# Sliding-window attention issued as 96 items, with row-tiled scores, one PSUM ring and the small transfers on SyncE

## The chip, the cores and the metric

The kernel runs on one core of one Trainium2 chip. The metric is the device time of one execution in microseconds, the median of several runs. The core has a matrix engine (TensorE, PE in the profile, with its weight loads as PEld), a vector engine (VectorE, DVE), an activation engine (ScalarE, ACT), GpSimd (POOL) and SyncE (SP), which here only issues DMA transfers. Each engine executes its own instructions in program order and waits on semaphores for the others.

## The reference

Two independent parts, each with 2048 positions and 576 channels, are computed and put side by side.

```python
# part A: 32 heads of 18, causal window of 256
qkv = (x @ wqkv).reshape(B, S, 3, H, Dh) ...          # q, k, v: [B, H, S, 18]
scores = einsum("bhqd,bhkd->bhqk", q, k) * Dh ** -0.5
mask = (i - j >= 0) & (i - j < 256)
p = softmax(where(mask, scores, -1e9))
a = einsum("bhqk,bhkd->bhqd", p, v) ... @ wo
# part B: a state-space filter with 128 states a channel, applied as a causal convolution by FFT
K[d, l] = real(sum_n C[d,n] * exp(dt * A[d,n] * l) * dt * B[d,n])
b = irfft(rfft(pad(u)) * rfft(pad(K)))[:L] + u * Dskip
out = concatenate([a, b], -1)
```

## The kernel before

The kernel has two stages. The first (to about 520 us) projects q, k and v (`proj`, written to `qd` and `vd` in HBM as pairs of f16 numbers that add up to one f32), builds the filter table K (`tables`) and makes the first half of the FFT of u and of K (`s1_u`, `s1_k`, written to `gx` and `gk` in HBM). The change does not touch it.

The second stage runs attention and the rest of the convolution side by side. Attention has 16 units: unit i is one half of the queries (1024) and one group of four heads. In a unit:

- `gmax_load` and `load_stacks` bring q, k and V from HBM. The f16 pairs are stacked on the partitions, so that one matmul of 54 rows and one further row computes a score with its row maximum taken off. The four heads lie side by side in a tile of 96 partitions.
- `gmax` finds an upper bound of each row's maximum: DVE spreads q into a block-diagonal tile `Qbd` (L580), PE multiplies 32 queries of four heads with 288 keys (L593) and adds a bias that hides the keys outside of the window (L596, L599), DVE reduces (L602 for a pair of two banks, L606 for the shorter ones). A transpose (L609) and a scaling (L611) turn the maxima into rows, and four transfers on POOL's queue (L613) put them into the tile Q.
- `att_chunk` computes, twice a unit, 512 queries: transposed scores of four heads (L634) in three banks of blocks listed in `BL`, the exponential on ACT (L636), the window's edges cut to zero on POOL (L645), and the products with V and a column of ones (L652), accumulated in `po`. DVE copies `po` into `osb` (L657).
- `norm` divides by the sum: transfers on POOL's queue gather the sums (`den`, L663), DVE inverts them (L664), they go out to HBM (`rd`, L666) and come back spread over partitions (`rb`, L669); DVE multiplies (L670), ACT and DVE split into an f16 pair (L672, L673), and POOL's queue stores it to `od` (L676).

The convolution (`conv`) has 16 passes over frequency pairs: loads, the second FFT half of u and K (L464), complex products on DVE (L486 to L489), sums (L494, L495), the inverse half (L497), a store to `h` on POOL's queue (L500). Then 16 steps of the last FFT (L517), each with four loads of `h` on SP, four of u and a product with Dskip on POOL, an addition on DVE (L519) and four stores. `wo` is the output projection (14 matmuls of 288 columns a tile, L151) and a scaling on ACT (L723); its first half may begin when units 0 to 7 are stored, its second when all are.

In the unit's loop, generators of attention, maxima of the next unit, convolution and projection are merged step by step (`merge`), with a share for each. What stands in the source is not yet the order on the engines: the compiler that the kernel is built with schedules the instructions once more before it fixes each engine's program, with pools of rotating buffers deciding what may overlap. Pools that matter: `sps` (maxima, one tile of two PSUM banks), `stp` (scores, one tile of two banks), `ops` (one bank, shared by `po` and the transpose), `fps` (three banks, convolution and projection), `P` (three tiles of exponentials).

Of the kernel before, what the change touches and what calls it, by code (L numbers as in the profile page):

```python
# [10 lines left out]
F32 = mybir.dt.float32  # L11
# [10 lines left out]
HQ = 1024  # L22
# [16 lines left out]
def constants():  # L39
# [33 lines left out]
    bd = np.zeros((96, 4))  # L73
    for j in range(4):
        bd[18 * j:18 * j + 18, j] = 1
    c["c_w1"], c["c_w2"], c["c_i1"], c["c_i2"] = w1, w2, i1, i2
    c["c_id"], c["c_bias"], c["c_bd"] = np.eye(128), bias, bd
# [14 lines left out]
def part(g, n):  # L92
    for _ in range(n):
        try:
            next(g)
        except StopIteration:
            return
        yield


class Kernel:
# [348 lines left out]
    def conv(self):  # L450
        nc, a, tt = self.nc, self.a, self.nc.vector.tensor_tensor
        fs, fy, fps = self.p["fs"], self.p["fy"], self.p["fps"]

        def gload(g, fp, nm, eng):
            t = fs.tile([128, 4, 2, 144], F32, name=nm)
            eng.dma_start(t, g.rearrange("a l (s f) j -> (a l) s f j", s=4)[:, :, 2 * fp:2 * fp + 2, :])
            return t

        def s2(w2, t, fp, hs):
            r = []  # L460
            for part in range(2):
                ps = fps.tile([128, 512], F32, name="fps")
                for par in range(2):
                    nc.tensor.matmul(ps[64 * par:64 * par + 64, :288], w2[:, par, 64 * part:64 * part + 64],  # L464
                                     t[:, 2 * hs:2 * hs + 2, par, :], start=True, stop=True)
                r.append(ps[:, :288])
            return r

        for fp in range(16):
            w2 = fs.tile([128, 2, 128], F32, name="w2")  # L470
            nc.sync.dma_start(w2, a["c_w2"][:, 2 * fp:2 * fp + 2])
            i1 = fs.tile([128, 2, 128], F32, name="i1")
            nc.sync.dma_start(i1, a["c_i1"][:, 2 * fp:2 * fp + 2])
            tx = gload(self.gx, fp, "tx", nc.sync)
            tk = gload(self.gk, fp, "tk", nc.sync)
            ho = fs.tile([128, 2, D], F32, name="ho")
            for hs in range(2):
                xr, xi = s2(w2, tx, fp, hs)
                X = fy.tile([128, 2, 288], F32, name="X")
                self.evac(X[:, 0], xr)  # L480
                self.evac(X[:, 1], xi)
                yield
                kr, ki = s2(w2, tk, fp, hs)
                t1 = fy.tile([128, 2, 288], F32, name="t1")
                t2 = fy.tile([128, 2, 288], F32, name="t2")
                tt(t1[:, 0], X[:, 0], kr, op=OP.mult)  # L486
                tt(t2[:, 1], X[:, 1], kr, op=OP.mult)  # L487
                tt(t2[:, 0], X[:, 1], ki, op=OP.mult)
                tt(t1[:, 1], X[:, 0], ki, op=OP.mult)  # L489
                yield  # L490
                for par in range(2):
                    Y = fy.tile([128, 288], F32, name="Y%d" % par)
                    sl = slice(64 * par, 64 * par + 64)
                    tt(Y[0:64], t1[sl, 0], t2[sl, 0], op=OP.subtract)  # L494
                    tt(Y[64:128], t1[sl, 1], t2[sl, 1], op=OP.add)  # L495
                    ps = fps.tile([128, 512], F32, name="fps")
                    nc.tensor.matmul(ps[:, :288], i1[:, par, :], Y, start=True, stop=True)  # L497
                    self.evac(ho[:, par, hs * 288:hs * 288 + 288], ps[:, :288])
                yield
# [3 lines left out]
        for qd in range(16):  # L503
# [5 lines left out]
            ut = fs.tile([128, D], F32, name="tx")  # L509
            y = fs.tile([128, D], F32, name="tk")  # L510
            for k in range(4):
                nc.gpsimd.dma_start(ut[32 * k:32 * k + 32], uw[4 * qd + k])
# [314 lines left out]
```

## Time and profile before

| | |
|---|---|
| median of 3 runs | 1375.21 us (1371.36 to 1375.58) |
| profiled execution | 1368.52 us, span 1366.8 us |
| mean granted PE clock | 0.828 |
| busy share of the span | PE 74%, PEld 39%, DVE 55%, ACT 44%, POOL 40% |

The span is the time from the first to the last instruction of the profiled execution; the execution took 1.7 us more. Busy time is the time in which an engine works on an instruction; matmuls are pipelined, and their ends are modelled, so busy PE is not PE at its peak. In a list of groups a row has line, engine, operation, output and input tile, shapes, count, then busy us and mean ns of one, then the idle time before them with what ended it. In a timeline or chain a row has start, duration, engine or queue, line and count. DMA transfers of SP have no landing time in this profile, those of POOL's queue have.

### The profile page before, as it was taken

How to read it: one execution, taken by the hardware profiler on the slowest of the kernel's cores; microseconds unless marked ns; L12 is line 12 of the kernel's file. 1: busy time of each engine (PE TensorE's matmuls, PEld its weight loads, DVE VectorE, ACT ScalarE, POOL GpSimd, SP SyncE). 2: the span in 40 equal slices, each digit the busy share in tenths (PEclk: the TensorE clock that was granted, in tenths of full speed). 3: DMA queues.
4: the chain of work that ended last, by engine and by line, in shares of the span. 5: the costliest groups of instructions: out<-in, count | busy, mean ns of one | idle time of the engine just before them, and what ended most of it. 6: DMA issues, size and time to landing. Idle time of an engine off the chain costs nothing.

```text
span 1366.8 us, 25524 instructions
## 1 busy us (share of the span) xinstructions
PE 1009.0 (74%) x10314; PEld 535.1 (39%) x10314; DVE 755.2 (55%) x1229; ACT 599.5 (44%) x879; POOL 549.1 (40%) x700
## 2 busy tenths in 40 slices
PE   1548898798889864876797789667888896666338
PEld 1224464464455532333343334333444453222116
DVE  4797667777753254566766677544555765411210
ACT  2867687687783320432343234422443352233002
POOL 0024343454450260244543354333534454576640
PEclk8659999999999986788888888757999997776559
DMA  9563142133125668144433444225344423434673
GB/s 269 141 181 103 34 116 75 54 75 98 50 56 153 168 179 229 52 128 113 125 117 107 127 125 146 84 65 143 87 114 137 140 75 109 105 88 118 160 177 130
DMA packets 155541, 162.34 MB, mean 119 GB/s; under 512 B 34752, under 2 KB 128512, under 8 KB 155232
## 3 DMA queue, kind: packets, MB, share of 16 engines
q1 hardware_dynamic: 138768, 128.65, 33.9%
q0 software_dynamic: 15152, 28.08, 7.2%
q10 hardware_dynamic: 1504, 3.99, 1.0%
q8 instruction: 81, 1.33, 0.4%
q14 instruction: 36, 0.29, 0.1%
HBM read 103.11 MB, written 57.15 MB: 117 GB/s over the span
## 4 chain that ended last, share of the span: by engine, by line
PE 43%; DVE 22%; DMA 14%; ACT 9%; issue 6%; POOL 5%; SPq 2%; ACTq 0%; DVEq 0%; POOLq 0%
PE po L652 7%; PE ST L634 6%; PE fps L464 5%; PE S L593 5%; PE pp L151 5%; DVE m L602 4%; DMA Q<-m 4%; PE fps L151 4%; ACT P L636 3%; PE fps L497 3%; PE kp L388 2%; PE pp L431 2%; DMA den<-osb 2%; DMA gk<-g 2%; DVE Qbd L580 2%
## 5 line engine op out<-in xcount | busy, mean ns | idle before, releaser
L636 ACT ACTIVATE P<-ST,esc 128x1024 f32<-128x1024 f32 (+1 forms) x192 | 203.5, 1060 | 270.3 <-PE ST L634 242.6
L602 DVE TENSOR_REDUCE m<-S 128x2 f32<-128x576 f32 x224 | 168.7, 753 | 163.1 <-PE S L596 161.4
L645 POOL TENSOR_SCALAR_AFFINE_SELECT P<-P 128x512 f32<-128x512 f32 x240 | 159.7, 695 | 199.5 <-ACT P L636 189.2
L350 POOL TENSOR_TENSOR m<-A,tr 128x1024 f32<-128x1024 f32 x72 | 149.5, 2098 | 193.5 <-PE kp L388 143.9
L593 PE MATMUL S<-kh,Qbd 96*128 96x288 f16 (+7 forms) x512 | 135.4, 323 | 87.4 <-DVE m L602 55.3
L634 PE MATMUL ST<-Q,K 96*128 96x384 f16 (+2 forms) x704 | 141.3, 320 | 65.4 <-ACT P L636 38.1
L652 PE MATMUL po<-P,V 128*32 128x256 f32 (+2 forms) x1408 | 132.9, 458 | 14.3 <-POOL P L645 13.1
L634 PEld LDWEIGHTS <-K 96*128 96x128 f16 x704 | 64.8, 108 | 150.5 <-issue 132.3
L388 PE MATMUL kp<-Q,m 128*32 128x64 f32 x4608 | 87.6, 229 | 27.5 <-DVE Q L371 10.5
L388 PEld LDWEIGHTS kp<-Q,m 128*32 128x32 f32 x4608 | 74.6, 115 | 55.6 <-issue 41.8
L593 PEld LDWEIGHTS <-Qbd 96*128 96x128 f16 x512 | 56.3, 111 | 97.1 <-issue 38.3
L596 PE MATMUL S<-bias,idb 128*128 128x64 bf16 x448 | 92.0, 216 | 0.0
L431 PE MATMUL pp<-ut,w 128*128 128x288 f32 x128 | 51.4, 526 | 42.2 <-DMA ut<-in_u_dram 24.9
L652 PEld LDWEIGHTS po<-P,V 128*32 128x32 f32 x1408 | 41.4, 122 | 82.1 <-issue 42.9
L596 PEld LDWEIGHTS <-idb 128*128 128x128 bf16 x448 | 47.9, 108 | 62.3 <-issue 59.3
L464 PE MATMUL fps<-tx,w 128*64 128x288 f32 x256 | 66.1, 456 | 0.0
L497 PE MATMUL fps<-Y,i 128*128 128x288 f32 x128 | 56.1, 537 | 11.1 <-DVE Y L495 6.3
L464 PE MATMUL fps<-tk,w 128*64 128x288 f32 x256 | 61.4, 430 | 0.4 <-DVE t L487 0.4
L517 PE MATMUL fps<-ho,i 128*64 128x288 f32 x128 | 29.7, 593 | 39.7 <-DMA ho<-h 33.3
L519 DVE TENSOR_TENSOR tk<-fps,tx 128x288 f32<-128x288 f32 x32 | 14.4, 457 | 73.6 <-PE fps L517 65.6
L114 ACT ACTIVATE X<-fps 128x288 f32<-128x288 f32 x64 | 25.8, 409 | 66.5 <-PE fps L464 62.1
L114 ACT ACTIVATE g<-pp 128x288 f32<-128x288 f32 (+1 forms) x84 | 34.5, 446 | 46.1 <-PE pp L431 25.3
(160 smaller groups left out, 1918.8 us busy)
## 6 DMA issues: line engine op xcount, KB each, us to landing
gx<-g SPq DMA_DIRECT2D x32, 288.0 KB
qd<-qst SPq DMA_DIRECT2D x36, 256.0 KB
gk<-g SPq DMA_DIRECT2D x16, 576.0 KB
tx<-gx SPq DMA_DIRECT2D x16, 576.0 KB
tk<-gk SPq DMA_DIRECT2D x16, 576.0 KB
h<-ho POOLq DMA_DIRECT2D x16, 576.0 KB, 3.6
ho<-h SPq DMA_DIRECT2D x64, 144.0 KB
raw<-in_xT_dram SPq DMA_DIRECT2D x16, 512.0 KB
```

What stands on the lines that cost most here:

```text
L151: self.nc.tensor.matmul(ps, u, v, start=(i == 0), stop=(i == len(ops) - 1))
L350: self.nc.gpsimd.tensor_tensor(m, A[:, ch, a0:a0 + 8].unsqueeze(3).to_broadcast(sh), tr[:, ch, part, 0:8].unsqueeze(2).to_broadcast(sh), o ...
L388: nc.tensor.matmul(kp[32 * st:32 * st + 32, c % 2 * JJ2 + j, :], m[:, ch, a0:a0 + 32], Q[:, ch, term % 2, :], start=(term == 0), stop=(ter ...
L464: nc.tensor.matmul(ps[64 * par:64 * par + 64, :288], w2[:, par, 64 * part:64 * part + 64], t[:, 2 * hs:2 * hs + 2, par, :], start=True, st ...
L497: nc.tensor.matmul(ps[:, :288], i1[:, par, :], Y, start=True, stop=True)
L593: nc.tensor.matmul(ps[:, u, :n[u]], bdt[:, t].rearrange("p j q -> p (j q)"), kh[:, k0:k1], start=True, stop=False, skip_group_check=True)
L596: nc.tensor.matmul(ps[:, u, :288].rearrange("p (a b) -> p a b", b=32)[:, 0:9:8], self.idb, self.bias, start=False, stop=True, skip_group_c ...
L602: nc.vector.tensor_reduce(m[:, 2 * sp:2 * sp + 2], ps[:, :, :n[0]], axis=AX.X, op=OP.max)
L634: nc.tensor.matmul(ps[:, u, o:o + n], d["K"][:, j, k0:k0 + 128], d["Q"][:, j, q0:q0 + n], start=True, stop=True, skip_group_check=True)
L636: nc.scalar.activation(pt[:, 2 * jp:2 * jp + 2, lo:hi], ps[:, :, lo:hi], AF.Exp, scale=self.esc)
L645: nc.gpsimd.affine_select(v, v, pattern=[[0, 4], [sg, 128]], compare_op=OP.is_ge, fill=0.0, base=-1 if far else 0, channel_multiplier=-sg)
L652: nc.tensor.matmul(po[32 * j:32 * j + 32, t0 * 128:t1 * 128], d["V"][:, kb * 76 + 19 * j:kb * 76 + 19 * j + 32], P[off // 512][:, j, o:o + ...
```

## The change

Attention becomes one generator, `attention`, that walks 96 items: one item is one bank of one chunk of one unit. In item n the scores of item n, the V products of item n-2, seven of the next unit's maxima steps, two or three of 225 smaller convolution steps and, from item 62, one projection step are merged. Besides:

- Scores are row-tiled: two heads lie in partitions 0 to 63 and 64 to 127, each with 64 rows, and the two matmuls of a pair use different halves of the rows and different banks. The number of score matmuls stays.
- `stp` has two tiles in place of one. `sps` and `fps` become one `ring` of three one-bank tiles for maxima, transpose, convolution and projection. `P` has four buffers, V three, `n` two.
- q is loaded straight into its block-diagonal tile, by four transfers with runs of 64 bytes, so DVE's spreading is gone; the reduces are all single (32 a unit).
- `po` is copied by ACT. `norm` yields twice, so that its steps lie an item apart.
- Transfers of the maxima, of `norm`, of `h` and of u go from POOL's queue to SP's. Convolution loads are issued one pass or one step ahead.
- Most of the memsets at the start of the stage move from POOL to DVE.

The core of the diff (the functions that only move text are left out):

```diff
     def gmax(self, i):
-        for sp in range(16):
-            ps = self.p["sps"].tile([128, 2, 512], F32, name="S")
...
+        for t in range(32):
+            ps = self.p["ring"].tile([128, 512], F32, name="r")
+            full = hf > 0 or t >= 8
+            k0 = 32 * t if full else 256
+            n = 32 * t + 288 - k0
+            nc.tensor.matmul(ps[:, :n], d["q"][:, t].rearrange("p j q -> p (j q)"), d["k"][:, k0:k0 + n],
+                             start=True, stop=False, skip_group_check=True)
...
+            nc.vector.tensor_reduce(m[:, t:t + 1], ps[:, :n], axis=AX.X, op=OP.max)
+            yield
+        yield
+        mt = self.p["ring"].tile([128, 512], F32, name="r")
         nc.tensor.transpose(mt[:32, :128], m, self.ident)
...
         for j in range(4):
-            nc.gpsimd.dma_start(d["Q"][64:65, j].rearrange("o (s q) -> o s q", q=32), m16[:, 32 * j:32 * j + 32])
+            r = 64 * (j % 2) + 54
+            nc.sync.dma_start(d["Q"][r:r + 1, j // 2].rearrange("o (s q) -> o s q", q=32), m16[:, 32 * j:32 * j + 32])
+    def scores(self, i, c, bank):
+        nc, d, bb = self.nc, self.sets[i % 2], self.blocks(i, c, bank)
+        pt = self.p["P"].tile([128, 4, 512], F32, name="P")
...
+        for jp in range(2):
+            ps = self.p["stp"].tile([128, 2, 512], F32, name="ST")
+            for off, r, t0, t1 in bb:
...
+                for u in range(2):
+                    h = slice(64 * u, 64 * u + 64)
+                    nc.tensor.matmul(ps[:, u, o:o + n], d["K"][h, jp, k0:k0 + 128], d["Q"][h, jp, q0:q0 + n],
+                                     start=True, stop=True, skip_group_check=True)
+            nc.scalar.activation(pt[:, 2 * jp:2 * jp + 2, lo:hi], ps[:, :, lo:hi], AF.Exp, scale=self.esc)
+            yield
...                                   # the window's edges on POOL, as before
+    def values(self, i, c, bank):
...                                   # the V products of one bank, as before
+        if bank == 2:
...
+            nc.scalar.activation(self.osb[i][:, c * 512:c * 512 + 512], self.po, AF.Copy)
+    def norm(self, i):
...                                   # as before, on nc.sync, with a yield after den and after rb
+    def attention(self, conv):
+        self.V, self.Pt, self.osb, norms = {}, {}, {}, []
+        self.load_unit(0)
+        for _ in self.gmax(0):
+            pass
+        items = [(i, c, b) for i in range(16) for c in range(2) for b in range(3)]
+        wo0 = self.wo(0)
+        for n in range(len(items) + 2):
+            streams = []
+            if n < len(items):
+                i = items[n][0]
+                if n % 6 == 0 and i < 15:
+                    self.load_unit(i + 1)
+                    gm = self.gmax(i + 1)
+                streams.append((self.scores(*items[n]), 2))
+                if i < 15:
+                    streams.append((part(gm, 7), 7))
+            if n >= 2:
+                streams.append((self.values(*items[n - 2]), 2))
+            k = conv_steps(n)                 # (n + 1) * 225 // 96 - n * 225 // 96
+            streams.append((part(conv, k), k))
+            if n == 24:
+                self.wo_load()
+            if n >= 62:
+                streams.append((part(wo0, 1), 1))
+            merge(*streams)
+            norms = [g for g in norms if next(g, 0) is None]
+            if n >= 2 and (n - 2) % 6 == 5:
+                norms.append(self.norm(items[n - 2][0]))
+                next(norms[-1])
...                                   # then the rest of norms, conv, wo0, and wo(1)
@@ build
-                for n, b, s in (("fs", 2, None), ("fy", 2, None), ("att", 1, None), ("bd", 1, None), ("m", 2, None),
-                                ("P", 3, None), ("v", 2, None), ("o", 2, None), ("n", 1, None), ("wo", 1, None),
-                                ("wo2", 2, None), ("sps", 1, PSUM), ("stp", 1, PSUM), ("ops", 1, PSUM),
-                                ("fps", 3, PSUM)):
+                for n, b, s in (("fs", 2, None), ("fy", 2, None), ("att", 1, None), ("m", 2, None), ("P", 4, None),
+                                ("v", 3, None), ("o", 2, None), ("n", 2, None), ("wo", 1, None), ("wo2", 2, None),
+                                ("stp", 2, PSUM), ("ops", 1, PSUM), ("ring", 3, PSUM)):
```

The convolution's steps become smaller (six instead of three yields for each half pass) and issue their loads first:

```diff
+        nx = load(0)
         for fp in range(16):
-            w2 = fs.tile([128, 2, 128], F32, name="w2")
...
+            cu, nx = nx, load(fp + 1) if fp < 15 else None
...
-            nc.gpsimd.dma_start(self.h.rearrange("a l f d -> (a l) f d")[:, 2 * fp:2 * fp + 2, :], ho)
+            nc.sync.dma_start(self.h.rearrange("a l f d -> (a l) f d")[:, 2 * fp:2 * fp + 2, :], ho)
...
+        nx = loadh(0)
+        yield
         for qd in range(16):
+            (hp, ut), nx = nx, loadh(qd + 1) if qd < 15 else None
```

More of the change, by code (lines that the diff above doesn't have):

```diff
@@ new lines, in ring, with s2 @@
+        def ring():
+            return self.p["ring"].tile([128, 512], F32, name="r")[:, :288]
+        def s2(w2, t, part, hs):
+            ps = ring()
+            for par in range(2):
+                nc.tensor.matmul(ps[64 * par:64 * par + 64], w2[:, par, 64 * part:64 * part + 64],
+                                 t[:, 2 * hs:2 * hs + 2, par, :], start=True, stop=True)
+            return ps
+        nx = load(0)
+        for fp in range(16):
+            cu, nx = nx, load(fp + 1) if fp < 15 else None
```

273 lines of the change are left out of this document (108 added, 165 removed).

## The prediction

> **What bounds the kernel now.** I read the page's span, then the windows, then PE's timeline for marks that cut the attention stage into units, and then the chain of waits inside one unit.
>
> ```profile
> span 1366.8 us, 25524 instructions
> 543.40:1227.60 684.20, 536.38 (x3839) 259.57 (x3839) 395.78 (x724) 248.04 (x307) 304.63 (x509) 0.82 0.39 109
> 543.37 0.39 PE L609 MATMUL po<-ident,m 128*32 128x128 f32 x1 [1.25 <-DVE m L602]
> 1227.61 0.28 PE L609 MATMUL po<-ident,m 128*32 128x128 f32 x1 [0.81 <-DVE osb L657]
> ```
>
> The transpose of the row maxima (L609) runs once a unit: fifteen cycles in 684.2 us, 45.6 us each. The columns after the length are PE, PEld, DVE, ACT, POOL, the clock and DMA. PE is busy 78% of it at 0.82 of the clock, DVE 58%, ACT 36%: no engine is full, so order and waits set the time. Two waits stand out, in the chain of a unit that has little else to do, and in the timelines of POOL and ACT at a unit's border.
>
> ```profile
> 1237.87 1.02 PE ST L634 x4
> 1238.92 1.12 ACT P L636
> 1240.08 1.02 PE ST L634 x4
> ...
> 849.80 2.06 POOL L663 DMA_DIRECT2D den<-osb  x4 [1.53 <-DVE V L560]
> 851.85 0.98 POOL L613 DMA_DIRECT2D Q<-m  x2
> 859.05 1.00 POOL L613 DMA_DIRECT2D Q<-m  x2
> 861.83 0.90 ACT L636 ACTIVATE P<-ST,esc 128x768 f32<-128x768 f32 x1 [9.02 <-PE ST L634]
> ```
>
> With one score buffer, scores and exponentials take turns, 2.2 us a round. At the border the four transfers of the maxima go out in two pairs 7 us apart, because the reciprocal and its transfer stand between them on POOL, and the first exponential starts 10 us after the first of them.
>
> **The order of the changed program.** The compiler reorders the streams, so I read the instruction order of the built program, which was not run. Up to the first maxima matmul PE's order is the same matmul for matmul: about 520 us are unchanged. After that it is not the fine interleave of the source. In nine of the fifteen cycles (0-1, 4-5 to 7-8, 10-11, 12-13, 13-14, 14-15) PE runs all scores and V products of a unit as one burst, then all 32 maxima matmuls of the next unit mixed with convolution, then the transpose, then the next burst. In the other six a large part of the two phases is mixed. On SP every DMA waits for the one eight before it.
>
> **The costs of one cycle.**
>
> ```profile
> L636 ACT ACTIVATE P<-ST,esc 128x1024 f32<-128x1024 f32 x160 | 178.1, 1113 | 220.6 <-PE ST L634 194.3 <-POOL P L645 15.3 <-PE po L652 9.7
> L645 POOL TENSOR_SCALAR_AFFINE_SELECT P<-P 128x512 f32<-128x512 f32 x240 | 159.7, 695 | 199.5 <-ACT P L636 189.2
> L606 DVE TENSOR_REDUCE m<-S 128x1 f32<-128x256 f32 x8 | 3.3, 412 | 0.0
> L486 DVE TENSOR_TENSOR t<-X,fps 128x288 f32<-128x288 f32 x32 | 14.5, 452 | 11.2 <-PE fps L464 10.5 <-ACT X L114 0.4
> L494 DVE TENSOR_TENSOR Y<-t,t 64x288 f32<-64x288 f32 x64 | 34.3, 536 | 1.0
> L116 DVE COPY ho<-fps 128x288 f32<-128x288 f32 x32 | 14.4, 450 | 7.2 <-PE fps L497 6.7
> 858.92 0.44 DVE L487 TENSOR_TENSOR t<-X,fps 128x288 f32<-128x288 f32 x1
> 859.28 0.45 DVE L488 TENSOR_TENSOR t<-X,fps 128x288 f32<-128x288 f32 x1
> ```
>
> *Burst.* The second score buffer lets exponentials follow each other: 12 x 1.113 = 13.4 us (units of the first half have eight full and four shorter or smaller ones, about 12). Behind them come the two osb copies, moved from DVE to ACT (512 columns, half an exponential: 1.2 us), the last three selects (3 x 0.695 = 2.1) and the last V products (0.5): 17.2 us, or 15.8. In the 2.2 us rounds 12 took 26. Row tiling hardly enters, because ACT is the bound:
>
> ```profile
> 1041.74 0.29 PE L593 MATMUL S<-kh,Qbd 96*128 96x288 f16 x1
> 1041.90 0.29 PE L593 MATMUL S<-kh,Qbd 96*128 96x288 f16 x1
> 1064.31 1.07 PE L652 MATMUL po<-P,V 128*32 128x256 f32 x16
> 1065.35 0.43 PE L634 MATMUL ST<-Q,K 96*128 96x128 f16 x3
> L464 PE MATMUL fps<-tx,w 128*64 128x288 f32 x256 | 66.1, 456 | 0.0
> L464 PE MATMUL fps<-tk,w 128*64 128x288 f32 x256 | 61.4, 430 | 0.4 <-DVE t L487 0.4
> L497 PE MATMUL fps<-Y,i 128*128 128x288 f32 x128 | 56.1, 537 | 11.1 <-DVE Y L495 6.3
> ```
>
> Sixteen V records take 1.04 us, so a unit's 96 take 6.2; 48 score matmuls of 256 columns, priced like the 288-column matmul and its small partner (0.16 us), take at most 7.7, or half if pairs run together. PE needs 10 to 14 us of the 17: the second half of row tiling is worth between 0 and 4 us a unit, and I book 0.
>
> *Maxima phase.* A single reduce of 288 columns is 0.445 us by the 256-column row; back to back, starts are 0.08 closer than durations (858.92 to 859.28), so 32 cost 11.7 us. One convolution pass costs DVE (4 x 14.5 + 2 x 34.3 + 14.4)/16 = 8.8, less 18 x 0.08: 7.4 us. DVE has 19.1 us. PE has 32 x 0.16 = 5.1 and (66.1 + 61.4 + 56.1)/16 = 11.5: 16.6 us. The three-tile ring lets PE run at most three tiles ahead, and convolution tiles sit in it too. Perfect cover gives 19, none 36; I take 23, near the DVE sum, because reduces wait in the ring while an add runs. The multiplications by the mask (L580) go, and the split reduces give that back.
>
> *Gap between the last reduce and the burst.*
>
> ```profile
> rb<-rd POOLq DMA_DIRECT2D x64, 128.0 KB, 2.8
> od<-oh POOLq DMA_DIRECT2D x64, 72.0 KB, 2.4
> Q<-m POOLq DMA_DIRECT2D x64, 2.0 KB, 4.7
> rd<-den POOLq DMA_DIRECT2D x16, 16.0 KB, 1.7
> ```
>
> Transpose, scaling and four DMAs remain, now on SP. In the built order rd (which waits for the reciprocal behind the scaling) and often the four rb stand among the four Q transfers. With nothing between it is 1 + 1.7 = 3 us; with rd and rb between, 1 + 1.7 + 2.8 + 1.7 and issue, about 9. The 4.7 of the Q row is nearest the middle: 1.7 us of transpose, scaling and issue plus 4.7 gives 6.4. Behind these waits on SP are the loads of the next unit, of which the maxima phase needs its part only after the burst (16 us later), so they are covered; in a gap twice as long they still are. POOL loses 64 issues each of den, Q, rb and od, and selects no longer stand behind them. The Trainium skill (DMA: Bandwidth & Descriptors, section SWDGE vs HWDGE vs iDMA and the table of latencies) gives a first byte after 1 us for descriptors made on GpSimd and 0.6 for SP's. By it the gap would be an estimated 0.4 us shorter, 6 us in fifteen cycles; no run here shows small transfers on SP yet.
>
> *Sum.* A cycle with separate phases is 23 + 6.4 + 16.5 = 46 us, what it is now: the burst's saving is spent on laying phases end to end. In a mixed cycle the phases share time and the gap has work over it: I take 37, between the longer phase with its gap (23 + 6.4 = 29) and 46. Nine times 46 and six times 37 are 636. Two separate cycles carry six or seven output-projection groups in their maxima phase, which makes PE the bound there: 12 us. In the last, 6.5 of the final FFT's 16 steps must load in time: at 5 us a step (below) 32 instead of 23, 9 us more. Together 657 against 684.2: 27 us gained.
>
> **Start and tail.**
>
> ```profile
> 526.23 0.76 DVE L602 TENSOR_REDUCE m<-S 128x2 f32<-128x576 f32 x1 [0.84 <-PE S L596]
> 527.82 0.76 DVE L602 TENSOR_REDUCE m<-S 128x2 f32<-128x576 f32 x1 [0.84 <-PE S L596]
> ...
> GB/s 269 141 181 103 34 116 75 54 75 98 50 56 153 168 179 229 52 128 113 125 117 107 127 125 146 84 65 143 87 114 137 140 75 109 105 88 118 160 177 130
> ...
> 1302.58 2.20 PE fps L517 x8
> 1309.79 2.20 PE fps L517 x8
> 1329.21 4.29 DMA oh<-od
> 1333.55 29.25 PE fps L151 x224
> ```
>
> Unit 0's maxima alone run 1.59 us a pair, reduce and matmul in turn. With the ring two singles take 0.8: twelve pairs save 9, and eight small ones begin among the last filter copies; the twelve memsets moved to DVE lie in the same stretch, where copies wait for loads, and cost up to 3. Gain 10 us.
>
> After the last transpose 139.2 us are spent now. Now each final-FFT step takes 7.2 us (1302.58 to 1309.79), as its loads follow the stores of the step before. Loaded one step ahead, a step costs half the load-compute-store loop, 5 us; its 1.15 MB need 4.3 at the best rate of the page (269 GB/s). After: 1 + 6 + 17.2 for the last burst, six steps of 5, then the norm of unit 15, whose reciprocal DVE now has behind the last step: 1.7 + 2.8 + 2.4 and issue, three passes of 1.1 to 1.4, and 4.3 for oh, about 19 us with PE idle; then 29.3 for the last projection and 3 to store. That is 106: 33 gained, although the norm, hidden now, comes into the open.
>
> The profiled execution took 1368.5 us for a span of 1366.8, and the median of the runs is 0.5% above it. 1366.8 - 10 - 27 - 33 = 1297, or 1298.5 executed, and 1305 as a median.
>
> **Rivals.**
>
> *The phases overlap after all.* If ring and buffers let bursts hide under the maxima phase, a cycle costs the DVE's 19.1 plus 4 for norm, osb off it, and loss: 33 us. 15 x 33 = 495, 189 gained instead of 27: about 1140. For it: no engine is over 80%. Against it: each engine keeps its program order, and in nine cycles that order is serial.
>
> *SP becomes the bound.* Some 41 DMAs a unit, in order, eight in flight. A small Q transfer behind two 576 KB convolution loads or a store that waits for DVE and ACT arrives late, and the burst, the ring and the next maxima wait with it. Each microsecond of gap costs 15. From 11 us a gap (4.7 more) the kernel is slower than before; at 13 it is 1405. For it: on POOL the pairs came 7 us apart; against it: these stores are issued early in the phase.
>
> *PE goes cold.*
>
> ```profile
> 520.00:560.00 40.00, 21.21 (x117) 10.42 (x117) 18.90 (x38) 4.61 (x6) 3.92 (x7) 0.56 0.53 146
> 1040.00:1080.00 40.00, 35.29 (x270) 18.52 (x272) 26.74 (x46) 17.75 (x22) 16.13 (x29) 0.96 0.36 105
> ```
>
> A stretch of maxima with little beside it ran at 0.56, a mixed one at 0.96. At 0.56 a burst's 10 to 14 us of PE become 18 to 25 against 17.2: 4 us more in nine cycles, and 3 in the maxima phase: 63 us, 1368. The Trainium skill (TensorE: Matmul & The Clock Gate, Part 1) says an idle window of 3.4 us halves the clock; the first row agrees in size, and the gaps here would be long enough.
>
> **How the numbers follow.** Forecast 0.50 (1250 to 1360: the phase 20 to 27, the gap 4 to 9); overlap 0.17 (1100 to 1250); SP 0.18 (1385 to 1450); cold PE 0.15 (1330 to 1410). About 0.3%, 4 us, is what a measurement can tell from no change. The last case splits: 0.06 faster, 0.03 same, 0.06 slower; so faster 0.73, same 0.03, slower 0.24. The range 1195 to 1400 leaves out about 0.1 at either end.
>
> **What would show it.** Right: transposes about 46 us apart in separate cycles and 37 in mixed ones; exponentials back to back in bursts; DVE idle in bursts and ACT in maxima phases; POOL without DMA rows; PE idle some 19 us before the last 224 matmuls. Wrong: equal cycles near 33; waits of PE for Q<-m above 10 us; a clock under 0.7 throughout.

## The result and the profile after

The changed kernel takes 1449.9 us (median of 4 runs, 1447.2 to 1455.0) against 1375.4 (1371.4 to 1381.7): ratio 1.054, 95% interval 1.049 to 1.059. The forecast was 1305, faster than before, within 1195 to 1400; it is wrong, in its direction too.

First the page of the changed kernel, its groups (line, engine, operation, count, then busy us and mean ns, then idle time before with what ended it), then the exponentials' row of the page before, and the window from the first to the last transpose of the maxima, which is line L605 now:

```profile
span 1445.5 us, 25772 instructions
...
L633 ACT ACTIVATE P<-ST,esc 128x1024 f32<-128x1024 f32 (+1 forms) x192 | 195.2, 1062 | 122.6 <-PE ST L631 121.5
...
L631 PE MATMUL ST<-Q,K 64*128 64x384 f16 (+2 forms) x704 | 104.0, 335 | 111.0 <-DMA Q<-m 67.2
...
L681 ACT ACTIVATE oh<-osb 128x1024 f16<-128x1024 f32 x16 | 16.9, 1054 | 144.6 <-DVE osb L679 121.1
...
L679 DVE TENSOR_TENSOR osb<-osb,rb 128x1024 f32<-128x1024 f32 x16 | 20.2, 1260 | 72.6 <-DMA rb<-rd 72.6
```

```profile
L636 ACT ACTIVATE P<-ST,esc 128x1024 f32<-128x1024 f32 (+1 forms) x192 | 203.5, 1060 | 270.3 <-PE ST L634 242.6
```

```profile
525.04:1322.05 797.01, 552.11 (x3868) 229.73 (x3868) 355.84 (x852) 259.58 (x337) 148.28 (x232) 0.78 0.39 103
```

What was to become cheaper did: idle time before the 192 exponentials fell from 270.3 to 122.6 us, and the scores' 704 matmuls take 104.0 us of PE (141.3 before). But the fifteen cycles take 797.0 us where they took 684.2, 53.1 each in place of 45.6, with every engine busy for a smaller share of it. The new idle rows say where: scores wait 67 us for the maxima's rows (Q<-m), the scaling product of `norm` (L679) 73 us for rb, and ACT's cast behind it (L681) 121 us for that product.

One border between two units shows how. The rows are of PE, DVE and SP (SPq: the issue of transfers), start and duration first:

```profile
654.47 0.28 PE L605 MATMUL r<-ident,m 128*32 128x128 f32 x1
...
657.30 1.61 PE L502 MATMUL r<-Y,i 128*128 128x288 f32 x4 [1.91 <-DVE Y L498]
668.16 0.82 PE L631 MATMUL ST<-Q,K 64*128 64x384 f16 x3 [9.25 <-DMA Q<-m]
...
673.82 0.69 PE L631 MATMUL ST<-Q,K 64*128 64x384 f16 x2 [2.25 <-DMA Q<-m]
```

```profile
655.30 0.27 DVE L607 TENSOR_SCALAR m<-r 32x128 f16<-32x128 f32 x1
...
658.13 0.35 DVE L672 RECIPROCAL den<-den 128x32 f32<-128x32 f32 x1
658.95 0.46 DVE L118 COPY ho<-r 128x288 f32<-128x288 f32 x1 [0.46 <-PE r L502]
666.57 1.23 DVE L679 TENSOR_TENSOR osb<-osb,rb 128x1024 f32<-128x1024 f32 x1 [7.17 <-DMA rb<-rd]
668.92 1.22 DVE L682 TENSOR_TENSOR oh<-osb,oh 128x1024 f16<-128x1024 f32 x1 [1.12 <-ACT oh L681]
```

```profile
658.52 0.32 SPq L674 DMA_DIRECT2D rd<-den  x1
...
660.00 2.00 SPq L677 DMA_DIRECT2D rb<-rd  x4
662.04 0.56 SPq L463 DMA_DIRECT2D tk<-gk  x1
662.64 2.18 SPq L610 DMA_DIRECT2D Q<-m  x3
670.17 1.40 SPq L685 DMA_DIRECT2D od<-oh  x4
671.62 0.51 SPq L610 DMA_DIRECT2D Q<-m  x1
672.17 2.14 SPq L571 DMA_DIRECT2D qh<-qd  x4
```

The maxima's rows are ready at 655.6 (the transpose and its scaling). They go out behind rd and rb, and the fourth of them behind od, which waits for the whole normalisation. DVE has one copy between reciprocal and scaling product, then stands 7.2 us for the rest of the round trip (rd to HBM, rb back). The next unit's loads (qh) stand behind it all on SP. Two convolution loads of 576 KB (tk is one) go out in between; how much of the round trip's length they make, no run tells.

By waits from 530 to 1230 us (us in total, times, longest) it is the same all along. The second fence has the kernel before, where the scaling product waited for rb once and DVE never for a V buffer (V is the tile of values; DVE sets its last columns to zero, L581, when PE is done with the buffer's last content, L654):

```profile
DVE V L581 <- PE po L654: 76.5, 8, 15.8
PE ST L631 <- DMA Q<-m: 64.6, 20, 11.3
DVE osb L679 <- DMA rb<-rd: 59.0, 10, 8.7
```

```profile
PE ST L634 <- DMA Q<-m: 21.4, 8, 4.4
...
DVE osb L670 <- DMA rb<-rd: 9.1, 1, 9.1
```

The prediction's sign of being wrong, a wait of PE for Q<-m above 10 us, is there: the longest is 11.3.

What the prediction's sums have no term for is the order of DVE's program. The built programs list how many DVE instructions lie between the reciprocal and the scaling product in units 0 to 15, that is, what can be done during the round trip:

```
before                24 25 22 22 22 23 20 11 13 11 14 19  6  0  5  2   sum 239
changed                9  1  0  8  0  0  5  0  0 22 10  5  0  7  2  0   sum  69
```

### The profile page after: what moved, and what is told of

Its sections match the earlier page's. It is cut to its first block, busy times and chain, and to the rows that moved or that the text cites. A ratio compares the mean times of both kernels' runs of the same rounds, so it can differ in the third digit from the quotient of the medians.

```text
span 1445.5 us, 25772 instructions
## 1 busy us (share of the span) xinstructions
PE 1010.0 (70%) x10314; PEld 499.5 (35%) x10314; DVE 712.5 (49%) x1369; ACT 610.8 (42%) x911; POOL 330.3 (23%) x340
## 4 chain that ended last, share of the span: by engine, by line
PE 36%; DVE 21%; DMA 13%; ACT 13%; SPq 7%; issue 6%; POOL 3%; POOLq 0%; DVEq 0%; ACTq 0%
PE po L654 6%; PE r L472 6%; ACT P L633 5%; PE r L153 4%; PE r L502 4%; PE r L593 4%; PE pp L153 3%; DVE m L601 3%; PE ST L631 3%; PE kp L390 2%; POOL P L642 2%; PE pp L433 2%; DMA rb<-rd 2%; DMA raw<-in_wo_dram 2%; DVE tr L330 1%
## 5 line engine op out<-in xcount | busy, mean ns | idle before, releaser
L601 DVE TENSOR_REDUCE m<-r 128x1 f32<-128x288 f32 (+7 forms) x512 | 198.4, 432 | 207.6 <-PE r L596 153.0
L633 ACT ACTIVATE P<-ST,esc 128x1024 f32<-128x1024 f32 (+1 forms) x192 | 195.2, 1062 | 122.6 <-PE ST L631 121.5
L631 PE MATMUL ST<-Q,K 64*128 64x384 f16 (+2 forms) x704 | 104.0, 335 | 111.0 <-DMA Q<-m 67.2
L593 PE MATMUL r<-kh,qh 96*128 96x288 f16 (+7 forms) x512 | 140.2, 313 | 43.7 <-DVE m L601 18.8
L654 PE MATMUL po<-P,V 128*32 128x256 f32 (+2 forms) x1408 | 146.6, 451 | 22.9 <-POOL P L642 18.1
L631 PEld LDWEIGHTS <-K 64*128 64x128 f16 x704 | 34.8, 102 | 204.4 <-issue 153.1
L593 PEld LDWEIGHTS <-qh 96*128 96x128 f16 x512 | 54.9, 108 | 108.2 <-issue 66.0
L596 PE MATMUL r<-bias,idb 128*128 128x64 bf16 x448 | 90.9, 210 | 0.0
L502 PE MATMUL r<-Y,i 128*128 128x288 f32 x128 | 62.9, 582 | 26.7 <-DVE Y L498 14.1
L681 ACT ACTIVATE oh<-osb 128x1024 f16<-128x1024 f32 x16 | 16.9, 1054 | 144.6 <-DVE osb L679 121.1
L529 PE MATMUL r<-ho,i 128*64 128x288 f32 x128 | 33.8, 644 | 60.0 <-DMA ho<-h 57.4
L116 ACT ACTIVATE X<-r 128x288 f32<-128x288 f32 x64 | 26.3, 411 | 104.5 <-PE r L472 104.2
L654 PEld LDWEIGHTS po<-P,V 128*32 128x32 f32 x1408 | 42.1, 117 | 78.9 <-POOL P L642 40.0
L596 PEld LDWEIGHTS <-idb 128*128 128x128 bf16 x448 | 46.3, 104 | 41.5 <-issue 34.7
L472 PE MATMUL r<-tx,w 128*64 128x288 f32 x256 | 55.1, 517 | 2.3 <-DVE m L601 1.1
L679 DVE TENSOR_TENSOR osb<-osb,rb 128x1024 f32<-128x1024 f32 x16 | 20.2, 1260 | 72.6 <-DMA rb<-rd 72.6
```

What stands on the lines that cost most here:

```text
L472: nc.tensor.matmul(ps[64 * par:64 * par + 64], w2[:, par, 64 * part:64 * part + 64], t[:, 2 * hs:2 * hs + 2, par, :], start=True, stop=True)
L502: nc.tensor.matmul(ps, cu["i1"][:, par, :], Y[par], start=True, stop=True)
L593: nc.tensor.matmul(ps[:, :n], d["q"][:, t].rearrange("p j q -> p (j q)"), d["k"][:, k0:k0 + n], start=True, stop=False, skip_group_check=True)
L596: nc.tensor.matmul(ps[:, :288].rearrange("p (a b) -> p a b", b=32)[:, 0:9:8], self.idb, self.bias, start=False, stop=True, skip_group_chec ...
L601: nc.vector.tensor_reduce(m[:, t:t + 1], ps[:, :n], axis=AX.X, op=OP.max)
L631: nc.tensor.matmul(ps[:, u, o:o + n], d["K"][h, jp, k0:k0 + 128], d["Q"][h, jp, q0:q0 + n], start=True, stop=True, skip_group_check=True)
```

## The experiments

The theories, under the numbers or letters that the expectations use: **1 or D**, PE's built order lays the phases end to end; **2 or B**, the queue itself: on SP every transfer stands behind the one that waits; **3 or C**, PE needs more time, by clock or tiling; **A**, the round trip of `norm` is uncovered in DVE's order; **E**, the queue acts through the orders that are built. Times are medians of 4 runs; the kernel before ran on the same chip each time (1374 to 1380).

**Order and queue, one at a time.** `pe_source_order` chains PE's instructions of the stage in the order of the source, `all_source_order` those of all five engines:

```diff
+                n0 = len(nc.cur_bb.bb.instructions)
                 self.attention(self.conv())
+                self.pin(n0, ("PE",))          # a dependency without a wait from each PE instruction to the next
```

> The changed kernel with PE's instructions from the start of the attention stage chained to the order of the source (issue order only, no added wait for results); the other engines are still ordered by the compiler. Theory 1 (the built order lays bursts and maxima phases end to end, and the Q transfers' way is bare between them): cycles fall from 53 us to 35 to 42, about 160 to 270 us less, 1180 to 1290 us. Theory 2 (the shared SP queue is the bound, whatever PE's order): cycles stay above 48, 1390 to 1450. Theory 3 (PE itself needs more time, by its clock or by changes of tiling between scores, products and convolution): no gain, 1430 to 1500, as the finer mixing has more such changes.

> As the PE order run, but all engines and SP chained to the order of the source in the attention stage. Theory 1: if the source's order is what was meant, as fast or faster than with PE alone, 1150 to 1290. Theory 2: SP in source order has the Q transfers ahead of the norm of the same item, so the gap is short too; if SP's in-order waits are the bound it is slower than the PE-only run by 20 to 60 us. Theory 3: 1430 to 1500.

Measured 1436.5 (ratio 1.045, 1.036 to 1.054) and 1461.8 (1.064, 1.057 to 1.071). Theory 1 alone falls: PE's phases are mixed now, and the time is nearly as long. PE waits for the unit's loads before the maxima's matmuls (waits of `pe_source_order` from 530 to 1230 us):

```profile
PEld L593 <- DMA K<-qd: 87.6, 9, 14.6
PE r L593 <- DMA kh<-qd: 68.5, 7, 14.4
PE r L593 <- DMA Q<-qd: 49.2, 4, 12.6
```

In `all_source_order` hardly anything waits for the round trip (DVE 16.0 us for rb and nothing for V, PE 0.8 for the maxima's rows), and yet it is the slower of the two. PE waits for loads there too, and 84.3 us for DVE's reduces, 47.3 of them in one piece: cycle 4-5 takes 93.5 us, where the source has the loading and scaling of the projection's weights (`wo_load`) in one block.

`q_on_pool` gives the four transfers of the maxima's rows back to POOL, `norm_on_pool` all those of `norm`, `h_on_pool` those of h and u:

```diff
-            nc.sync.dma_start(d["Q"][r:r + 1, j // 2]...      # q_on_pool
+            nc.gpsimd.dma_start(d["Q"][r:r + 1, j // 2]...
-            nc.sync.dma_start(den[32 * j:32 * j + 32]...      # norm_on_pool: den, rd, rb, od
+            nc.gpsimd.dma_start(den[32 * j:32 * j + 32]...
```

> The changed kernel with only the four Q transfers of a unit back on POOL's queue, where nothing else is queued but the selects. Theory 2 (Q transfers stand behind rb and od on SP): the wait of the first scores after a transpose falls from 10 to 15 us to about 6 in cycles 2, 3, 8, 9, 11 and 14, 40 to 60 us less in all, 1390 to 1410. Theory 1 gives the same in these cycles but leaves the rest at 50: it does not pass below 1380. Theory 3: within 10 us of 1450.

> The changed kernel with the transfers of the norm (den, rd, rb, od) on POOL's queue, Q transfers on SP. Theory 2: Q transfers no longer wait for the norm, and the rb transfers no longer wait behind convolution loads: 60 to 100 us less, 1350 to 1390, but selects wait on POOL for the norm again, which gives back up to 2 us a unit. Theory 1: gain only through the order that the compiler makes of it, which mixes more units: 1330 to 1400. Theory 3: within 10 us of 1450.

> The changed kernel with only h (the convolution's results to memory) and u issued by POOL. SP waits 162 us for ho in the changed kernel. Theory B: the loads and the maxima's rows behind it come sooner: 1400 to 1435. Theory A, and also that this wait is idle time of SP that nobody feels: 1440 to 1455.

Measured 1422.5 (1.035, 1.028 to 1.042), 1398.3 (1.018, 1.010 to 1.026) and 1456.6 (1.059, 1.055 to 1.064). The first two pay, 27 and 52 us; h does not, though SP waited 162 us for ho: a long wait on SP says nothing until someone is late behind it. Each of these kernels has its own built order, so 27 and 52 us are the price of queue and order together. In `norm_on_pool` PE waits 14.6 us for the maxima's rows in place of 64.6, but DVE still waits for rb:

```profile
DVE osb L679 <- DMA rb<-rd: 69.7, 10, 12.7
...
PE ST L631 <- DMA Q<-m: 14.6, 18, 3.3
...
DVE V L581 <- PE po L654: 7.3, 3, 5.5
```

DVE's waits for V fell from 76.5 to 7.3 us as well. That they cost time is not shown: in `h_on_pool` they are 128.0 us, and the time is that of the changed kernel within the intervals.

**That wait alone.** `norm_pool_no_wait`, on top of `norm_on_pool`:

```diff
-        nc.vector.tensor_tensor(osb, osb, rb, op=OP.mult)
+        nc.vector.tensor_tensor(osb, osb, self.one, op=OP.mult)     # a constant tile of ones
```

> Base: the changed kernel with the normalisation's transfers on POOL (1398 us). On top of that the product that scales osb takes a constant tile of ones instead of rb, so VectorE no longer waits for the round trip den -> rd -> rb; every transfer is still issued. The division by the sum is left out. Theory A (uncovered wait: the order built for VectorE puts the scaling product right behind the reciprocal, so VectorE stands still for the round trip, 70 us over the phase, and with it the maxima and PE): 1315 to 1345. Theory B (shared SP queue: what costs is that the running maximum's rows reach Q late): as its base, 1385 to 1400. Theory C (PE itself needs the time, by clock and tiling): 1385 to 1400.

The kernel leaves out the division by the sums. Measured 1355.0 (0.986, 0.980 to 0.992): 43 us less than its base, between the expectations of A and B. The 69.7 us of waits for rb are gone, but the orders were built anew: DVE now waits 46.3 us for den (20.9 in the base) and 24.9 for V (7.3), and 64 instructions lie between reciprocal and product (113). So this run supports A without giving the price of the wait: how much of the 43 us is the wait and how much the other order, it does not tell.

**The whole queue part.** `norm_q_on_pool` and `small_all_on_pool` put `norm` and the maxima's rows, then h and u too, on POOL.

> The changed kernel with both the normalisation's transfers and the four transfers of the maxima's rows on POOL, as before; only h, u and the loads stay on SP. In the order built for it, 13 or so VectorE instructions stand between reciprocal and scaling product in ten of the sixteen units (in the changed kernel and with the normalisation alone on POOL mostly none to three). Theory B: the two gains of the single moves (27 and 52 us) at most add up: 1370 to 1400. Theory A: the wait for rb is covered too, so more than the sum: 1320 to 1360. Theory C: 1385 to 1400.

> The changed kernel with the queue part of the change undone altogether: the maxima's rows, den, rd, rb, od, h and u are issued by POOL as before; all else stays changed. Theory B (one SP queue on which every transfer stands behind the one that waits): SP's waits for ho, 225 us where the normalisation and the maxima's rows are off it, go too, and the loads behind them come sooner: 1290 to 1340, about what was forecast for the whole change. Theory A (uncovered wait of VectorE for rb): nothing more to gain than with those two (1359 us): 1345 to 1375.

Measured 1358.9 (0.990, 0.984 to 0.996) and 1345.4 (0.978, 0.972 to 0.984). So all the rest of the change together is worth 2%, and the queue part costs 105 us of 1450. The 2% lie outside of the cycles: in `small_all_on_pool` the first transpose comes at 526.9 us (543.4 before) and the stretch after the last takes 109.4 (139.2), but the fifteen cycles take 714.5 us, less than the 797.0 of the changed kernel and more than the 684.2 before. In their built programs 314 and 287 DVE instructions lie between reciprocals and scaling products, 69 in the changed kernel's (in the first of the two mostly 23 to 30 a unit, not the 13 of its expectation): the queue of a transfer changes what order is built for other engines. `before_small_on_sp` does the queue part alone, on the kernel before:

```diff
-            nc.gpsimd.dma_start(...)           # Q<-m, den, rd, rb, od, h, u
+            nc.sync.dma_start(...)
```

> The kernel before, with one part of the change alone: the small transfers (maxima's rows, den, rd, rb, od, h, u) issued by SP instead of POOL. In the order built for it, 5 to 20 VectorE instructions still stand between reciprocal and scaling product, and the maxima's rows mostly stand ahead of the normalisation's on SP. Theory B (an own queue is what was lost): slower by the 79 us that the two moves gave back, less what the better places on the queue save: 1410 to 1455. Theory A (the missing cover, not the queue): 1365 to 1390. Theory C: 1370 to 1380.

Measured 1477.3 (1.076, 1.069 to 1.082): 102 us slower, more than either theory had. Here 256 instructions lie in between, so A cannot be the reason. Nor is it all attention: in the profiled execution the fifteen cycles are 61.6 us longer than before and the stretch after the last transpose 53.3. There PE waits 69.0 us for u, whose loads stand on SP too now and which only the changed kernel issues a step ahead.

**Queue against order.** Two kernels exchange the orders: the PE, VectorE and ScalarE programs of one built kernel are forced on the other by chains of dependencies without waits, and SP and POOL are left free. A third holds the kernel before to its own orders with the small transfers on SP.

```diff
+                self.hold(n0)      # chains PE, DVE and ACT in a stored order, that of the other built program
```

> The changed kernel, all its small transfers on SP, but PE, VectorE and ScalarE held to the orders that were built for the kernel with the normalisation and the maxima's rows on POOL (1359 us). Theory E (the queue acts through the orders that are built): 1340 to 1385. Theory B (the queue itself: transfers and loads standing on SP behind one that waits): 1420 to 1470.

> The converse: the normalisation's transfers and the maxima's rows on POOL, but PE, VectorE and ScalarE held to the orders that were built for the changed kernel (1450 us). Theory E: 1420 to 1455. Theory B: 1350 to 1390.

> The kernel before with its small transfers on SP (1477 us), but PE, VectorE and ScalarE held to the orders that were built for the kernel before (1375 us). Theory E: 1370 to 1400. Theory B: 1440 to 1490.

| us | orders built for SP | orders built for POOL |
|---|---|---|
| changed, `norm` and maxima's rows on SP | 1449.9 | 1402.4 |
| changed, the two on POOL | 1461.9 | 1358.9 |
| before, small transfers on SP | 1477.3 | 1443.2 |
| before, small transfers on POOL | not run | 1375 |

Neither B nor E holds alone. With the orders built for SP, a queue of their own brings `norm` and the rows nothing (1449.9 and 1461.9). With the better orders it is worth 44 us, and the orders are worth 48 us on SP and 103 on POOL. In the kernel before, the queue itself costs 68 us with orders held, and the orders the other 34. The waits of `queue_pool_orders_of_sp` (530 to 1230 us) show why: the three rows are no shorter than the changed kernel's, though the transfers have a queue of their own. They go with the orders.

```profile
DVE V L608 <- PE po L681: 87.8, 9, 17.0
DVE osb L706 <- DMA rb<-rd: 86.0, 11, 10.4
PE ST L658 <- DMA Q<-m: 66.4, 25, 7.3
```

And `before_sp_orders_held` shows the queue with the three engines' orders as before. In its profiled execution, the slowest of the four and 86 us longer than that of the kernel before, 52.6 us lie in the cycles and 27.8 behind the last transpose. Seven of its fifteen cycles take 40 to 44 us, eight 48 to 66. One of the long ones, on SP, then PE, then SP's waits from 1040 to 1098 us:

```profile
1064.75 1.40 SPq L717 DMA_DIRECT2D od<-oh  x4
...
1076.38 1.15 SPq L704 DMA_DIRECT2D den<-osb  x2
1077.62 2.43 SPq L654 DMA_DIRECT2D Q<-m  x4
...
1088.68 0.60 SPq L497 DMA_DIRECT2D tx<-gx  x1
```

```profile
1097.71 2.15 PE L505 MATMUL fps<-tx,w 128*64 128x288 f32 x6 [21.02 <-DMA tx<-gx]
```

```profile
SPq L717 <- DVE oh L714: 13.9, 1, 13.9
SPq L704 <- DVE V L601: 9.1, 1, 9.1
```

SP stood 13.9 us at od, which waits for the normalisation, and 9.1 at den, which waits for DVE; the loads behind them (V, Q, K, qh, kh and the convolution's) went out after 1081, and PE stood 21 us for tx.

**A version that beats both.** `pe_source_early_loads` has `norm` on POOL, PE in source order, one more item in each of the two gaps between the steps of `norm`, and qh and kh of unit i+2 loaded in the middle of unit i:

```diff
+                if n % 6 == 3 and i < 14:
+                    self.load_qk(i + 2)            # the loads of qh and kh, taken out of load_unit
                 streams.append((self.scores(*items[n]), 2))
...
-        yield
+        for _ in range(2):                         # in norm, after den and after rb
+            yield
```

> PE kept in the order of the source, normalisation's transfers on POOL with two more items between its steps, and the loads of the maxima's operands (qh, kh) of unit i+2 issued in the middle of unit i. With PE in source order alone (1436 us) the maxima began 19 us into a cycle because PE waited for loads (98, 79 and 49 us over the phase). Theory A and the loads as the cause there: cycles of about 40 us, 1220 to 1300. Theory C (PE needs the time): cycles of 48 to 50, 1350 to 1400. Theory B: Q's rows, still on SP, come in time once the normalisation is off SP: 1300 to 1380.

Measured 1293.7 us (0.941, 0.936 to 0.947), so theory C falls. Its window from the first to the last transpose, and its waits (530 to 1230 us):

```profile
525.03:1162.70 637.67, 486.34 (x3811) 198.13 (x3811) 361.68 (x852) 261.27 (x334) 249.59 (x410) 0.85 0.48 129
```

```profile
DVE osb L685 <- DMA rb<-rd: 15.5, 4, 12.1
...
PE ST L635 <- DMA Q<-m: 5.0, 5, 2.9
```

Cycles 3 to 9 take 35.3 to 37.2 us. What carries it was tested by taking one thing out or adding one:

> The 1294 us kernel (normalisation on POOL with two more items between its steps, qh and kh loaded half a unit earlier) without the source order on PE. Theory D (serial built order): without the order the maxima again stand after the scores: 1340 to 1380. Theory B (loads behind waiting transfers are all): the order doesn't matter: 1285 to 1310.

> The 1294 us kernel without the early loads: qh and kh of the next unit are issued at the head of the unit again; PE stays in source order, the normalisation on POOL with two more items between its steps. If PE's wait for qh and kh at the head of each cycle is what made PE in source order slow (226 us over the phase with all on SP): 1340 to 1410. If the order and the queue are enough: 1290 to 1320.

> The 1294 us kernel (PE in source order, qh and kh half a unit earlier, two more items between the normalisation's steps) with the normalisation's transfers left on SP. Theory E: with PE's order held the queue costs little: 1290 to 1325. Theory B: SP waits for den and oh as in the changed kernel and the loads stand behind: 1360 to 1420.

> The 1294 us kernel with VectorE and ScalarE held to the source order as well as PE. If the built orders of these two still hide waits better than the source's: 1300 to 1340. If they are where the remaining 45 us cycles come from: 1260 to 1290.

> The 1294 us kernel with the maxima's rows, h and u issued by POOL as well. Theory B: SP's waits for ho (131 us) and m (67 us) go; the cycles with the projection and the last transforms (63, 48, 67 us) shorten: 1240 to 1285. If POOL, which does the masks too, becomes late with the maxima's rows: 1290 to 1320.

| kernel | us | ratio to before | against 1293.7 |
|---|---|---|---|
| without the order on PE (`early_loads_built_order`) | 1448.1 | 1.054 (1.049 to 1.059) | +154 |
| without the early loads (`order_without_early_loads`) | 1340.9 | 0.974 (0.969 to 0.979) | +47 |
| `norm` on SP again (`early_loads_norm_on_sp`) | 1345.8 | 0.977 (0.971 to 0.982) | +52 |
| DVE and ACT in source order too (`order_on_three_engines`) | 1338.8 | 0.972 (0.966 to 0.978) | +45 |
| maxima's rows, h and u on POOL too (`all_together`) | 1302.0 | 0.947 (0.942 to 0.951) | +8 |

All three parts count. The +47 of the loads is the cleanest of them, since DVE, ACT and POOL run the same orders in both traces. The +52 of the queue, between what E and B had, goes with another order on DVE (100 instructions between reciprocal and product, against 259). The longer gaps in `norm` were not taken out by themselves. Order on PE brought 13 us to the changed kernel, with intervals that overlap, and 154 here; that it pays here because the other waits are gone is argued and fits the rows, but the order of the other engines changes with it. Without it the norm is uncovered again (112 instructions, against 259), ACT and DVE stand, and PE behind them; both expectations for that run were too low (waits from 540 to 1300 us):

```profile
ACT oh L687 <- DVE osb L685: 143.5, 10, 21.0
PE r L597 <- DVE m L605: 134.5, 19, 20.4
...
DVE osb L685 <- DMA rb<-rd: 81.3, 9, 14.5
```

The loss with DVE and ACT in source order is nearly all in one cycle: 4-5 takes 82.1 us in place of 36.1, where `wo_load` stands in one block as in `all_source_order`, ACT waits 36.0 us for the weights' loads and PE 43.5 in one piece for a reduce. The other fourteen cycles take 610.0 us in place of 601.6, though the sum of instructions in between falls from 259 to 175; so the run says little against the source order of these two elsewhere. And giving POOL the other small transfers too brings nothing: 8 us more, with intervals that overlap.

## Why the prediction was wrong, step by step

**Up to the first transpose: right.** It came at 525.0 in place of 543.4: 18 us gained, 10 forecast.

**The costs of one cycle: the step that failed.** By kinds of cycles, from the starts of L605:

| cycles | booked | measured |
|---|---|---|
| separate, nothing besides (0-1, 4-5 to 7-8) | 5 x 46 = 230 | 249 |
| separate, with projection or last FFT (10-11, 12-13 to 14-15) | 4 x 46 + 12 + 9 = 205 | 250 |
| mixed (1-2 to 3-4, 8-9, 9-10, 11-12) | 6 x 37 = 222 | 298 |
| sum | 657 | 797 |

The step summed each phase from the engine's own work and the gap from the maxima's four transfers. It goes by the built order of PE; nothing in it counts DVE's, where the normalisation's round trip had lost its cover: the 59 us that DVE stands for rb are no term of the sum, nor is SP's wait for od with rows and loads behind it. The experiments give these two a price only together with the orders: with the queue part undone the cycles take 714.5 us, so 82.5 of the missing 140 go with it. The other 57.5 stay without it, and their cause is open.

The gap of 6.4 us was right for separate cycles (transpose to first exponential 3.7 to 10.1 us, 6.2 in the mean) and wrong for the mixed ones: 10.2 to 15.3, 13.1 in the mean. More than half of the miss, 76 us, is in these six. "The gap has work over it" was the wrong sentence: the maxima's rows stood behind rd and rb, and in the border shown behind od. From the first exponential to the last V product separate cycles took 19.5 us, 16.5 booked. Seven cycles of the fastest version come near the 37 us of a mixed cycle, so the size can be reached, with rows and loads in time and a covered `norm`; it was not reached in the order that was built. The cycles with projection or last FFT took 36.6 us from the last V product to the next transpose, 23 to 32 booked; what held them was not taken apart.

"They are covered; in a gap twice as long they still are", of the loads behind on SP, fell where it was tested: with PE in source order their lateness was PE's main wait, and issuing two of them (qh and kh) earlier gave 47 us in the fastest version.

**The tail: a term of half its size.** 123.4 us, 106 forecast, 139.2 before. A step of the last FFT was booked at 5 us; four of the last five take 8.0 to 8.5, longer than the 7.0 to 7.2 of the last four before, since each still waits for its loads:

```profile
1364.86 2.19 PE L529 MATMUL r<-ho,i 128*64 128x288 f32 x8 [6.04 <-DMA ho<-h]
...
1411.53 2.83 PE L153 MATMUL r<-woh,oh 128*128 128x288 f16 x11 [22.31 <-DMA oh<-od]
```

The chain of the changed kernel shows why: it runs over SP, which issues four stores (L534), four loads of h, four of u and here four transfers of `norm` (L670) one behind the other, sixteen in the 8.1 us from one step's first store to the next step's:

```profile
1349.98 0.33 SPq L534
...
1355.51 0.55 SPq L670
...
1358.05 0.52 SPq L534
```

Loads one step ahead don't help where SP's own issuing is what takes the time. The prediction had no term for it, and the loads of u were put on SP by the change. The idle stretch ahead of the last projection was 22.3 us (19 forecast), and that projection 30.4 (29.3).

**The rivals.** "SP becomes the bound" had the sign and a range (1385 to 1450) whose last microsecond holds the result; that is partly luck, since its mechanism is half of it. The rows do stand behind a waiting store, and SP does bound the last FFT's steps. But the queue costs 44 us with the better orders, 68 in the kernel before, and nothing with the orders that were built for it: there the orders make the loss. "The phases overlap" (33 us a cycle) needed what `pe_source_early_loads` adds, where seven cycles in a row take 35.3 to 37.2. "PE goes cold" is not tested. Its sign, a clock under 0.7 throughout, is not there: the mean clock of the phase fell from 0.82 to 0.78, and PE's busy time in it rose by 15.7 us, where the phase grew by 112.8, although its work on scores fell; no run holds the clock. Row tiling, booked at 0, took the scores' matmuls from 141.3 to 104.0 us of PE; no run took it out alone.

**Open.** Why the compiler builds less cover when the transfers are on SP was not asked; that it does is read from its programs and tested by exchanging them. Open too is why the cycles take 30 us more than before even with the queue part undone. In the fastest version the cycle where the projection starts (63 us) and the last one (67) were left as they are.

## What to carry to other kernels

Where a compiler orders the streams, read the built program of every engine, not of the busiest alone: count what stands between the start of a round trip and the instruction that waits for it. A transfer that waits for compute can hold up the next unit's loads on the same queue: here od and den did, and h, with the longest waits of all on SP, did not. So test which one does, or issue the loads ahead of it. Test order and queue together, since an edit to one builds the other anew: here the order on PE alone gave 13 us, hardly clear of noise, the queue part alone 105, and order, `norm`'s queue and earlier loads 156. And look for one long cycle before a sum is explained by all of them.

## What the runs showed of the hardware

PE's clock falls and recovers within one border. Windows of the changed kernel around the border shown, the clock third from the end:

```profile
640.00:655.00 15.00, 14.22 (x117) 5.84 (x113) 12.17 (x31) 3.60 (x6) 2.02 (x3) 1.00 0.14 49
658.00:668.00 10.00, 0.77 (x3) 0.30 (x2) 2.14 (x4) 0.58 (x2) 0.00 (x0) 0.58 0.69 186
668.00:680.00 12.00, 6.69 (x36) 1.82 (x36) 1.22 (x1) 6.35 (x8) 1.85 (x4) 0.50 0.45 96
680.00:695.00 15.00, 14.20 (x123) 5.64 (x120) 8.28 (x23) 7.50 (x9) 6.61 (x11) 1.00 0.21 46
```

Behind the wait of 9 us the next 12 us run at 0.50, with PE half busy, and then at 1.00. The fall comes early: if the clock goes from 1.00 to 0.50 in the stretch from 658, its mean of 0.58 leaves 1.6 us at 1.00, so it fell by about 659.6, under a microsecond after PE's last matmuls (657.30 to 658.91), which followed 1.9 us of idle time. The Trainium skill (TensorE: Matmul & The Clock Gate, Part 1) says that an idle window of some 3.4 us halves the clock; the rows agree on the half, but show no whole 3.4 us of idle time ahead of the fall. A late transfer can so be paid twice, once as the wait and once as the slow stretch behind it; the second payment is not told apart by a run. Over the phase the clock was 0.82 before, 0.78 after and 0.85 in the fastest version.

SP's time to issue the same transfers differs from place to place. The four qh transfers with runs of 64 bytes kept SP 2.1 us at the border above (0.5 each), and in the fastest version, right behind the projection's loads, 6.4 us; why was not tested:

```profile
925.43 6.39 SPq L585 DMA_DIRECT2D qh<-qd  x4
```
